# Soft-capped attention and a soft mixture of experts on one core: where casts, loads and weight transfers are placed

## The chip, the cores and the metric

The kernel runs on one core of a Trainium2 chip. Its engines are TensorE (PE, matmuls, with a weight-load row of its own, PEld), VectorE (DVE), ScalarE (ACT), GpSimd (POOL) and SyncE (SP), which here only issues DMAs. Matmuls write PSUM, everything else works on SBUF. The metric is device time of one execution in microseconds, the median over several runs. The profile comes from one further execution and has its own time.

## The reference

Attention with a soft cap on the scores, over q, k and v of shape (8, 12, 448, 64), then a soft mixture of 8 experts with 4 slots each over the 3584 resulting rows of 768:

```python
scores = cap * np.tanh((q @ k.T / 8) / cap)          # cap = 30
attn = softmax(scores, axis=-1)
x = (attn @ v) as (3584, 768)
logits = x @ phi                                      # phi (768, 32)
d = softmax(logits, axis=0)                           # over all rows
slots = (d.T @ x) as (8, 4, 768)
h = np.maximum(slots[e] @ w1[e], 0)                   # w1 (8, 768, 1024)
slot_out[e] = h @ w2[e]                               # w2 (8, 1024, 768)
out = softmax(logits, axis=1) @ slot_out              # (3584, 768), f32
```

All inputs are float32; the kernel's matmuls work on bfloat16.

## The kernel before, in words

**Units.** A quad is four heads of one batch element (24 quads, Q = 0 to 23); a pair is two heads (48), and each pair has 7 tiles (64 keys of each of its two heads against 448 queries), so 336 tiles. A chunk j holds 6 tiles (56 chunks), a half chunk 3. Seven chunks make one batch element, called b, with three quads 3b, 3b+1, 3b+2.

**The order is written out by hand.** Each engine runs its instructions in the order in which the Python code issues them. The loop at L451 runs over the chunks. In chunk j ScalarE does two tanh (`tanh_chunk`, L243, one for each half chunk) and the exp of the chunk before (`exp_chunk`, L247); TensorE does the scores of the next chunk (`qk_chunk`, L236, two half chunks, into two PSUM buffers) and the probability-times-V passes of an earlier pair (`pv_pass`, L264, two halves), normalized by VectorE (`norm`, L274 and L275). One chunk in seven has no P·V pass. Between these stand the slots "0", "a", "b", "c", "d", in which `run` calls whatever `at(j, slot, f, ...)` has entered:

- `cast` (L194): VectorE turns a float32 q or k quad into bfloat16, and then SP issues the load of the next quad into the same buffer (`load`, L153; one buffer each for q, k and v).
- `transp` (L204, L206): seven TensorE transposes into the one buffer of `psT` and a VectorE copy out.
- `vcast` (L214, L215): GpSimd casts v into one of two buffers `vbd`, and SP issues the next v load.
- `x_transp`, `logits`, `slot_sums`, `e_transp`, `e_norm`, `e_sums`: the mixture's logits and slot sums of finished batch elements.
- `spare(n)`: n junk matmuls, whose result nobody reads, into the P·V buffer (one buffer).
- `load_w1`, `load_w2`: GpSimd issues a weight DMA that casts float32 to bfloat16. 24 jobs bring w1 into SBUF (512 KB each as bfloat16, three per expert), 6 bring the first 24 blocks of w2 into SBUF (768 KB), and 10 bring the other 40 blocks into a bfloat16 copy in DRAM, `w2d` (768 KB). They are entered at equal distances in chunks, L421.

`quad_in` (L386) enters the five steps of a quad: cast k, cast q, transpose k, transpose q, cast v.

**Start.** `load_first` issues quad 0 in halves, then v of quad 0, then k, q, v of quad 1 into an area that a w1 tile uses later. 33 junk matmuls run, then `first_half(0)` casts and transposes the first pair of quad 0, `qk_chunk(0)` follows, then `first_half(1)` and `qk_chunk(1)`.

**End.** After the last exp the attention's SBUF pools are closed and the tiles `w2t` (L535 to L539) take their place: 20 DMAs on SP's queue bring `w2d` back, each as soon as the attention tile under it is free. The built program gives SP eight completion semaphores in turn, so a DMA also waits for the landing of the one eight before. Layer 1 (L552), its transposes (`h_transp`) and layer 2 (L579) follow. Layer 2 takes 64 blocks for the first 384 output columns (half 0), casts the sums (L618), then 64 blocks for the second half, with five output tiles' first halves between (`half_tile`, L604), and casts these (L626). Then come the output matmuls (L642), scaled by VectorE or ScalarE (L646, L648) and stored (L594).

Of the kernel before, what the change touches and what calls it, by code (L numbers as in the profile page):

```python
# [9 lines left out]
BF16 = mybir.dt.bfloat16  # L10
# [4 lines left out]
P = 128  # L15
HP = 64
NT = 7
# [6 lines left out]
VW = 2 * (DH + 1)  # L24
# [4 lines left out]
def kernel(  # L29
# [12 lines left out]
    B, H, _, _ = q.shape  # L42
    D = H * DH
    E = moe_w1.shape[0]
    F = moe_w1.shape[2]
    NS = moe_phi.shape[1]
    NJ = D // P
    NFT = F // P
    cap = float(cap)
    qk_scale = 1.0 / (DH ** 0.5)  # L50
# [5 lines left out]
    NCH = NTILE // CH  # L56
    R2 = 24

    ctx.enter_context(tc.manual_schedule())
    pe, dve, act, pool, sp = nc.tensor, nc.vector, nc.scalar, nc.gpsimd, nc.sync  # L60
# [15 lines left out]
    pool.memset(mask[0:HP, NG - 1, :], MASKED)  # L76
    phib = consts.tile([P, NJ, NS], BF16, name="phib")
    ET4 = consts.tile([P, B // 2, NT, 2, HP], BF16, name="ET4")
    winv = consts.tile([P, B // 2, NT], F32, name="winv")
    hpad = consts.tile([P, E, NFT, NS], BF16, name="hpad")  # L80
    slT = consts.tile([P, NJ, NS], BF16, name="slT")
    zacc = consts.tile([P, 1], F32, name="zacc")
    rz = consts.tile([P, 1], F32, name="rz")
    slacc = consts.tile([P, NJ, NS], F32, name="slacc")

    w1b = [wts.tile([P, NJ, F], BF16, name=f"w1b{e}", tag="w1", bufs=E)
           for e in range(E - 1)]
    w2b = wts.tile([P, R2, D], BF16, name="w2b")


    blocks = [(i, ft, gg) for i in range(E // 4) for ft in range(NFT) for gg in range(4)]

    def w2_src(n0, n):

        i, ft, gg = blocks[n0]
        return bass.AP(tensor=moe_w2.tensor,
                       offset=((4 * i + gg) * F + ft * P) * D,
                       ap=[[D, P], [F * D, n], [1, D]])
# [8 lines left out]
    def load_w2(dst, n0):  # L107
        pool.dma_start(out=dst, in_=w2_src(n0, 4))

    wjobs = [(load_w1, e, jh) for e in range(E) for jh in range(NJ // 2)]  # L110
    wjobs += [(load_w2, w2b[:, n0:n0 + 4, :], n0) for n0 in range(0, R2, 4)]

    dram = ctx.enter_context(tc.tile_pool(name="dram", bufs=1, space=bass.MemoryType.DRAM))
    w2d = []
    for n0 in range(R2, len(blocks), 4):
        t = dram.tile([P, 4, D], BF16, name=f"w2d{n0}")
        wjobs.append((load_w2, t, n0))
        w2d.append(t)

    att = ExitStack()  # L120
# [1 line left out]
    cst = att.enter_context(tc.tile_pool(name="cst", bufs=1))  # L122
    ldv = att.enter_context(tc.tile_pool(name="ldv", bufs=1))
    qk = att.enter_context(tc.tile_pool(name="qk", bufs=2))
    vb = att.enter_context(tc.tile_pool(name="vb", bufs=1))
    exps = att.enter_context(tc.tile_pool(name="exps", bufs=4))
    xs = att.enter_context(tc.tile_pool(name="xs", bufs=4))
    attp = ExitStack()
    psS = attp.enter_context(tc.tile_pool(name="psS", bufs=2, space=PSUM))
# [3 lines left out]
    raws, casts, qkT = {}, {}, {}  # L133
# [3 lines left out]
    def quad_ap(nm, Q, h=None):  # L137
        b, hq = divmod(Q, NQB)
        off = (b * H + 4 * hq) * S * DH
        if h is not None:  # L140
            return bass.AP(tensor=srcs[nm].tensor, offset=off + 2 * h * S * DH,
                           ap=[[NT * DH, P], [1, NT * DH]])
        return bass.AP(tensor=srcs[nm].tensor, offset=off,
                       ap=[[NT * DH, P], [2 * S * DH, 2], [1, NT * DH]])
# [11 lines left out]
    def load_first():  # L156

        for nm in "qkv":
            raws[nm, 0] = raw_tile(nm)
        for h in range(2):  # L160
            sp.dma_start(out=raws["q", 0][:, h, :], in_=quad_ap("q", 0, h))
            act.dma_start(out=raws["k", 0][:, h, :], in_=quad_ap("k", 0, h))
        sp.dma_start(out=raws["v", 0], in_=quad_ap("v", 0))
        t = wts.tile([P, 3, 2, S], F32, name="raw1", tag="w1", bufs=E)
        for n, nm in enumerate("kqv"):
            raws[nm, 1] = t[:, n, :, :]
            sp.dma_start(out=raws[nm, 1], in_=quad_ap(nm, 1))

    def first_half(h):

        for nm in ("q", "k"):
            if h == 0:
                casts[nm, 0] = cst.tile([P, NT, P], BF16, name=nm + "bf", tag=nm + "bf")
                qkT[nm, 0] = qk.tile([P, NT, P], BF16, name=nm + "T", tag=nm + "T")
            dve.tensor_copy(
                casts[nm, 0][:, :, h * HP:(h + 1) * HP]
                .rearrange("p c (a d) -> p a c d", a=2),
                raws[nm, 0][:, h, :].rearrange("p (c a d) -> p a c d", a=2, d=DH // 2))
        for nm in ("q", "k"):
            ps = (psT if nm == "q" else psV).tile(  # L180
                [P, NT, P], BF16, name=nm + "ps", tag="T" if nm == "q" else "pv")
            r = slice(h * HP, h * HP + HP)
            for c in range(NT):
                pe.transpose(ps[r, c, :], casts[nm, 0][:, c, r], ident)
            cuts = (0, 2, NT) if (nm, h) == ("k", 0) else (0, NT)
            for c0, c1 in zip(cuts, cuts[1:]):
                dve.tensor_copy(qkT[nm, 0][r, c0:c1, :], ps[r, c0:c1, :])
            if h == 1:
                raws.pop((nm, 0)), casts.pop((nm, 0))
                load(nm, 2)  # L190
# [15 lines left out]
        dve.tensor_copy(t, ps)  # L206
        qkT[nm, Q] = t

    vbds = [vb.tile([P, 2, NT, VW], BF16, name=f"vbd{n}") for n in range(2)]

    def vcast(Q):
        raw = raws.pop(("v", Q)).rearrange("p h (c d) -> p h c d", d=DH)
# [14 lines left out]
    def qk_chunk(i):  # L227
        sc = psS.tile([P, CS, 512], F32, name="sc", tag="sc")
        scores[i] = sc
        for u in range(CS):  # L230
            pr, c = divmod(i * CS + u, NT)
            Q, h = divmod(pr, 2)
            r = slice(h * HP, h * HP + HP)
            for n in range(2):
                cs = slice(n * HP, n * HP + HP)
                pe.matmul(sc[cs, u, 0:S], qkT["k", Q][r, c, cs],  # L236
                          qkT["q", Q][r, :, cs], start=True, stop=True)
# [136 lines left out]
    def at(j, slot, f, *a):  # L374
        if j < 0:
            j, slot = 0, "b"
        aux.setdefault((j, slot), []).append((f, a))

    def spare(n):

        busy(n, psV.tile([P, 2, VW], F32, name="junk", tag="pv")[:, 0, 0:P])
# [4 lines left out]
    def quad_in(Q, cast_k, cast_q, k_in, q_in, v_in):  # L386
        if 0 < Q < NQ:
            at(*cast_k, cast, "k", Q)
            at(*cast_q, cast, "q", Q)
            at(*k_in, transp, "k", Q)  # L390
            at(*q_in, transp, "q", Q)
            at(*v_in, vcast, Q)

    for b in range(B):
        j = b * PER
        quad_in(3 * b + 1, (j - 1, "d"), (j, "a"), (j, "b"), (j, "c"), (j + 2, "c"))
        quad_in(3 * b + 2, (j + 1, "c"), (j + 1, "d"), (j + 2, "b"), (j + 2, "c"),
                (j + 5, "c"))
        quad_in(3 * b + 3, (j + 3, "d"), (j + 4, "c"), (j + 5, "b"), (j + 5, "c"),
                (j + 7, "c"))  # L400
        p = 6 * b
        at(j + 2, "a", spare, 12)
        at(j + 4, "a", x_transp, p)
        at(j + 5, "a", x_transp, p + 1)
        at(j + 6, "a", x_transp, p + 2)
        at(j + 5, "d", logits, 3 * b)
        if b < B - 1:
            at(j + 7, "a", x_transp, p + 3)
            at(j + 8, "a", x_transp, p + 4)
            at(j + 7, "d", logits, 3 * b + 1)  # L410
            at(j + 9, "a", x_transp, p + 5)
            at(j + 9, "d", logits, 3 * b + 2)
            at(j + 11, "0", e_exp, b)
            at(j + 11, "d", slot_sums, b)
            at(j + 12, "d", e_transp, b)
            at(j + 13, "d", e_norm, b)
            if b % 2:
                at(j + 14, "d", e_sums, b // 2)
    nw = len(wjobs)
    for n, job in enumerate(wjobs):  # L420
        at(1 + n * (NCH - 5) // nw, "b", *job)  # L421

    def run(j, slot):
        for f, a in aux.pop((j, slot), []):
# [12 lines left out]
    init_vbd()  # L437
    first_half(0)
    qk_chunk(0)
    first_half(1)  # L440
    qk_chunk(1)
    at(1, "b", vcast, 0)
    at(3, "b", dve.memset, hpad, 0.0)
    pool.dma_start(out=phib, in_=moe_phi.rearrange("(jt ji) s -> ji jt s", ji=P))
# [87 lines left out]

    tl = ctx.enter_context(tc.tile_pool(name="tl", bufs=1, reuse_waits="tile"))

    w2t = []  # L535
    for n0 in range(R2, len(blocks), 2):
        t = tl.tile([P, 2, D], BF16, name=f"w2t{n0}")
        sp.dma_start(out=t, in_=w2d[(n0 - R2) // 4][:, (n0 - R2) % 4:(n0 - R2) % 4 + 2, :])
        w2t.append(t)  # L539

    def w2_block(n):
        return w2b[:, n, :] if n < R2 else w2t[(n - R2) // 2][:, (n - R2) % 2, :]

    hbs = {}

# [24 lines left out]
                      ap=[hpad.ap[0], [NS, NFT], [NFT * NS + 4, 4], [1, 4]])  # L570
        dve.tensor_copy(dst, src)

    HD = D // 2
    so_ps = []

    def layer2(n0, half):
        for n in range(n0, n0 + 4):
            i, ft, gg = blocks[n]
            pe.matmul(so_ps[half][32 * gg:32 * gg + NS, :],  # L579
                      hpad[:, 4 * i + gg, ft, :],  # L580
                      w2_block(n)[:, half * HD:(half + 1) * HD],
                      start=(n0 == 0), stop=(n0 == len(blocks) - 4))

    layer1(0, 0, e_norm)
# [46 lines left out]
    for n in range(B // 2 * NT):  # L631
        bb, c = divmod(n, NT)
# [52 lines left out]
```

## Time and profile before

| | |
|---|---|
| median of 7 runs | 339.37 us (334.57 to 344.61) |
| profiled execution, whole | 337.23 us |
| its span, first to last instruction | 335.4 us |
| mean granted TensorE clock in it | 0.885 |
| ScalarE tanh, L243 | x112, 145.4 us busy, 1409 ns mean |
| ScalarE exp, L247 | x57, 144.0 us busy, 2546 ns mean |
| TensorE P·V, L264 | x1288, 98.6 us busy |
| TensorE scores, L236 | x672, 87.7 us busy |
| TensorE idle before score matmuls, for a PSUM buffer that ScalarE reads | 13.0 us in 24 waits |
| VectorE idle before q casts, for q loads | 4.4 us |
| DMA of w1, w2 (SBUF), w2 (DRAM) | x24, x6, x10; median 8.6, 10.7, 11.5 us to landing |
| DMA of q, k, v | x22, x22, x23; median 6.1, 5.6, 7.8 us to landing |
| reload of w2 from DRAM | x20, 384 KB each, median 5.8 us to landing |
| stores of whole output tiles | x23, 384 KB each, median 4.3 us to landing |

Durations on ScalarE include the overlap of an instruction with the one behind it, so two tanh and one exp together advance the timeline by 4.67 us a chunk, less than the sum of their means. In the slices of the page each character is 8.4 us: a digit is a share in tenths, and PEclk is the granted clock of TensorE, which in this execution is either 1.00 or 0.50 at any moment. In timelines the bracket at the end of a row tells how long the engine was idle before it and what ended that.

### The profile page before, as it was taken

How to read it: one execution, taken by the hardware profiler on the slowest of the kernel's cores; microseconds unless marked ns; L12 is line 12 of the kernel's file. 1: busy time of each engine (PE TensorE's matmuls, PEld its weight loads, DVE VectorE, ACT ScalarE, POOL GpSimd, SP SyncE). 2: the span in 40 equal slices, each digit the busy share in tenths (PEclk: the TensorE clock that was granted, in tenths of full speed). 3: DMA queues.
4: the chain of work that ended last, by engine and by line, in shares of the span. 5: the costliest groups of instructions: out<-in, count | busy, mean ns of one | idle time of the engine just before them, and what ended most of it. 6: DMA issues, size and time to landing. Idle time of an engine off the chain costs nothing.

```text
span 335.4 us, 8116 instructions
## 1 busy us (share of the span) xinstructions
PE 279.2 (83%) x3486; PEld 187.7 (56%) x3486; DVE 173.9 (52%) x426; ACT 282.5 (84%) x199; POOL 84.5 (25%) x107
## 2 busy tenths in 40 slices
PE   7789987999799887888998878978997887978680
PEld 6346664676557665665576556755665657533220
DVE  6624664356436654565366545754675345216542
ACT  2688999989979999999999999999999997203450
POOL 5500442234044231430442143341430220000000
PEclk9557999579959999999599999999899999989855
DMA  8992699394978995969799999999999553945998
GB/s 266 264 274 94 156 243 267 76 280 105 257 202 189 197 250 191 229 169 241 214 227 241 287 277 213 261 259 267 289 231 226 187 166 93 359 196 202 394 399 322
DMA packets 43044, 77.65 MB, mean 231 GB/s; under 512 B 3456, under 2 KB 31360, under 8 KB 43008
## 3 DMA queue, kind: packets, MB, share of 16 engines
q1 hardware_dynamic: 26960, 51.45, 43.8%
q0 software_dynamic: 15760, 25.22, 42.6%
q8 instruction: 27, 0.44, 0.5%
q10 hardware_dynamic: 288, 0.46, 0.4%
q14 instruction: 9, 0.07, 0.1%
HBM read 91.32 MB, written 18.87 MB: 329 GB/s over the span
## 4 chain that ended last, share of the span: by engine, by line
ACT 48%; PE 30%; DMA 9%; DVE 8%; issue 1%; SPq 1%; DVEq 0%; ACTq 0%
ACT ex L243 24%; ACT ex L247 23%; PE pv L264 8%; PE sc L236 8%; DMA qraw<-in_q_dram 5%; DMA out_dram<-ob 2%; DMA w2t<-w2d 2%; PE kps L204 2%; PE qps L204 2%; DVE kT L206 2%; PE so_ps L579 1%; PE hp L552 1%; PE boot L434 1%; SPq L594 1%; DVE xq L275 1%
## 5 line engine op out<-in xcount | busy, mean ns | idle before, releaser
L243 ACT ACTIVATE ex<-sc 128x1344 bf16<-128x1344 f32 x112 | 145.4, 1409 | 13.4 <-PE sc L236 10.7
L247 ACT ACTIVATE ex<-ex 128x2688 bf16<-128x2688 bf16 (+1 forms) x57 | 144.0, 2546 | 0.0
L264 PE MATMUL pv<-vbd,ex 128*128 128x130 bf16 x1288 | 98.6, 231 | 4.9 <-ACT ex L247 2.3
L264 PEld LDWEIGHTS <-ex 128*128 128x128 bf16 x1344 | 85.2, 103 | 26.3 <-DVE xq L275 17.1
L236 PE MATMUL sc<-qT,kT 64*64 64x448 bf16 x672 | 87.7, 395 | 13.4 <-ACT ex L243 13.0
L214 POOL CAST vbd<-vraw 64x896 bf16<-64x896 f32 x23 | 21.7, 944 | 147.1 <-DMA vraw<-in_v_dram 89.3
L274 DVE RECIPROCAL rec<-pv 128x4 f32<-128x4 f32 x92 | 16.8, 182 | 69.3 <-PE pv L264 69.3
L236 PEld LDWEIGHTS <-kT 64*64 64x64 bf16 x672 | 29.1, 111 | 34.5 <-issue 19.1
L275 DVE TENSOR_TENSOR xq<-pv,rec 128x256 bf16<-128x256 f32 x92 | 39.0, 424 | 3.2
L215 POOL CAST vbd<-vraw 64x896 bf16<-64x896 f32 x23 | 26.1, 1136 | 1.3
L206 DVE COPY kT<-kps 128x896 bf16<-128x896 bf16 x23 | 14.3, 622 | 16.4 <-PE kps L204 16.3
L194 DVE CAST qbf<-qraw 128x896 bf16<-128x896 f32 x22 | 19.1, 869 | 4.4 <-DMA qraw<-in_q_dram 4.4
L204 PE MATMUL qps<-ident,qbf 128*128 128x128 bf16 x161 | 14.1, 233 | 7.3 <-DVE kT L206 7.2
L292 DVE COPY xT<-xps 128x512 bf16<-128x512 bf16 x47 | 19.5, 415 | 1.0 <-PE xps L290 1.0
L290 PE MATMUL xps<-ident,xq 128*128 128x128 bf16 x188 | 18.5, 221 | 0.7 <-DVE zacc L329 0.7
L642 PE MATMUL op<-so,ET 128*128 128x384 bf16 x46 | 14.7, 416 | 4.8 <-DVE ob L646 3.4
L204 PEld LDWEIGHTS <-kbf 128*128 128x128 bf16 x161 | 10.8, 102 | 13.7 <-issue 8.6
L206 DVE COPY qT<-qps 128x896 bf16<-128x896 bf16 x23 | 14.3, 620 | 7.5 <-PE qps L204 7.2
L204 PE MATMUL kps<-ident,kbf 128*128 128x128 bf16 x161 | 13.9, 231 | 5.0 <-DVE xT L292 3.8
L648 ACT ACTIVATE ob<-op,winv 128x768 f32<-128x768 f32 x11 | 9.9, 900 | 9.5 <-DMA out_dram<-ob 8.0
L318 POOL COPY e<-E 128x512 bf16<-128x512 bf16 x8 | 4.9, 608 | 51.6 <-ACT E L312 36.1
L204 PEld LDWEIGHTS <-qbf 128*128 128x128 bf16 x161 | 12.0, 104 | 9.4 <-issue 9.0
(94 smaller groups left out, 224.2 us busy)
## 6 DMA issues: line engine op xcount, KB each, us to landing
w1b<-in_moe_w_dram POOLq DMA_DIRECT2D x24, 512.0 KB, 8.6
vraw<-in_v_dram SPq DMA_DIRECT2D x23, 448.0 KB, 7.8
qraw<-in_q_dram SPq DMA_DIRECT2D x22, 448.0 KB, 6.1
kraw<-in_k_dram SPq DMA_DIRECT2D x22, 448.0 KB, 5.6
out_dram<-ob SPq DMA_DIRECT2D x23, 384.0 KB, 4.3
w2d<-in_moe_w_dram POOLq DMA_DIRECT2D x10, 768.0 KB, 11.5
w2t<-w2d SPq DMA_DIRECT2D x20, 384.0 KB, 5.8
w2b<-in_moe_w_dram POOLq DMA_DIRECT2D x6, 768.0 KB, 10.7
```

The costliest lines, as they stand in the source:

```text
L194: dve.tensor_copy(t.rearrange("p c (h d) -> p h c d", h=2), raws.pop((nm, Q)).rearrange("p h (c d) -> p h c d", d=DH))
L204: pe.transpose(ps[:, c, :], src[:, c, :], ident)
L206: dve.tensor_copy(t, ps)
L214: pool.tensor_copy(t[0:HP, :, :, 0:DH], raw[0:HP])
L215: pool.tensor_copy(t[HP:P, :, :, DH + 1:VW - 1], raw[HP:P])
L236: pe.matmul(sc[cs, u, 0:S], qkT["k", Q][r, c, cs], qkT["q", Q][r, :, cs], start=True, stop=True)
L243: act.activation(exs[j][:, half * CS:half * CS + CS, :], scores.pop(i)[:, :, 0:S], ACT.Tanh, scale=qk_scale / cap)
L247: act.activation(exs[j][:, u0:u1, :], exs[j][:, u0:u1, :], ACT.Exp, scale=cap)
L264: pe.matmul(pvs[pr, half][:, n, 0:VW], exs[j][:, u, GOFF[g]:GOFF[g] + P], vbds[Q % 2][:, h, c, :], start=(c == 0 and n == 0), stop=(c == N ...
L275: dve.tensor_tensor(xq[Q][:, 2 * half:2 * half + 2, h * P:(h + 1) * P] .rearrange("p g (i d) -> p g i d", i=2), pv[:, :, :, 0:DH], rec.to_ ...
L290: pe.transpose(ps[:, g, :], xq[Q][:, g, h * P:(h + 1) * P], ident)
L292: dve.tensor_copy(t, ps)
```

## The change

- The start issues `qk_chunk(1)` ahead of `first_half(1)`, with six junk matmuls behind it. Ten more junk matmuls stand in each of the slots (0, "c"), (0, "d"), (1, "a") and (1, "c").
- v of quad 0 is loaded after k and q of quad 1.
- The steps of the three quads of a batch element move. For quad 3b+2, for example, cast k stays at (j+1, "c"), cast q moves from (j+1, "d") to (j+2, "c"), transpose k stays at (j+2, "b"), transpose q moves from (j+2, "c") to (j+2, "d"), and the v cast from (j+5, "c") to (j+4, "d").
- Weight jobs get costs 4 (w1), 6 (w2 to SBUF) and 3 (half of a w2 job to DRAM), and are entered in proportion to the costs, from chunk 2 on and not from chunk 1.
- Each of the 10 jobs to DRAM becomes two, one for each half of the output columns, and `w2d` holds the halves apart. The reload takes all first halves, then all second halves: still 20 DMAs of 384 KB.
- The two `vbd` buffers get pools of their own, with the `exps` pool between them in SBUF.

```diff
+    def load_half(dst, n0, half):
+        src = w2_src(n0, 4)
+        pool.dma_start(out=dst, in_=bass.AP(tensor=src.tensor, offset=src.offset + half * HD,
+                                            ap=[[D, P], [F * D, 4], [1, HD]]))
...
     for n0 in range(R2, len(blocks), 4):
-        t = dram.tile([P, 4, D], BF16, name=f"w2d{n0}")
-        wjobs.append((load_w2, t, n0))
+        t = dram.tile([P, 2, 4, HD], BF16, name=f"w2d{n0}")
+        for half in range(2):
+            wjobs.append((load_half, t[:, half, :, :], n0, half))
         w2d.append(t)
...
-    vb = att.enter_context(tc.tile_pool(name="vb", bufs=1))
+    vb = [att.enter_context(tc.tile_pool(name="vb0", bufs=1))]
     exps = att.enter_context(tc.tile_pool(name="exps", bufs=4))
+    vb.append(att.enter_context(tc.tile_pool(name="vb1", bufs=1)))
...
-        sp.dma_start(out=raws["v", 0], in_=quad_ap("v", 0))
         t = wts.tile([P, 3, 2, S], F32, name="raw1", tag="w1", bufs=E)
         for n, nm in enumerate("kqv"):
             raws[nm, 1] = t[:, n, :, :]
+            if nm == "v":
+                sp.dma_start(out=raws["v", 0], in_=quad_ap("v", 0))
             sp.dma_start(out=raws[nm, 1], in_=quad_ap(nm, 1))
...
-        quad_in(3 * b + 1, (j - 1, "d"), (j, "a"), (j, "b"), (j, "c"), (j + 2, "c"))
-        quad_in(3 * b + 2, (j + 1, "c"), (j + 1, "d"), (j + 2, "b"), (j + 2, "c"),
-                (j + 5, "c"))
-        quad_in(3 * b + 3, (j + 3, "d"), (j + 4, "c"), (j + 5, "b"), (j + 5, "c"),
-                (j + 7, "c"))
+        quad_in(3 * b + 1, (j - 1, "b"), (j, "a"), (j - 1, "d"), (j, "c"), (j + 1, "d"))
+        quad_in(3 * b + 2, (j + 1, "c"), (j + 2, "c"), (j + 2, "b"), (j + 2, "d"),
+                (j + 4, "d"))
+        quad_in(3 * b + 3, (j + 4, "a"), (j + 5, "a"), (j + 4, "d"), (j + 5, "c"),
+                (j + 6, "d"))
...
-    nw = len(wjobs)
+
+    cost = [{load_w1: 4, load_w2: 6, load_half: 3}[job[0]] for job in wjobs]
     for n, job in enumerate(wjobs):
-        at(1 + n * (NCH - 5) // nw, "b", *job)
+        at(2 + sum(cost[:n]) * (NCH - 6) // sum(cost), "b", *job)
+    for j, slot in ((0, "c"), (0, "d"), (1, "a"), (1, "c")):
+        at(j, slot, spare, 10)
...
     qk_chunk(0)
+    qk_chunk(1)
+    spare(6)
     first_half(1)
-    qk_chunk(1)
...
-    w2t = []
-    for n0 in range(R2, len(blocks), 2):
-        t = tl.tile([P, 2, D], BF16, name=f"w2t{n0}")
-        sp.dma_start(out=t, in_=w2d[(n0 - R2) // 4][:, (n0 - R2) % 4:(n0 - R2) % 4 + 2, :])
-        w2t.append(t)
...
+    w2t = {}
+    for half in range(2):
+        for n0 in range(R2, len(blocks), 4):
+            t = tl.tile([P, 4, HD], BF16, name=f"w2t{n0}_{half}")
+            sp.dma_start(out=t, in_=w2d[(n0 - R2) // 4][:, half, :, :])
+            w2t[n0, half] = t
...
+    def w2_half(n, half):
+        if n < R2:
+            return w2b[:, n, half * HD:(half + 1) * HD]
+        return w2t[n - n % 4, half][:, n % 4, :]
```

## The prediction

> **What bounds the kernel now.** I read the page first, then ScalarE's timeline (the busiest engine), then the windows by granted clock, then the chain of waits behind chunk 55. From the page, busy shares and the 40 slices of 8.4 us:
>
> ```profile
> PE 279.2 (83%) x3486; PEld 187.7 (56%) x3486; DVE 173.9 (52%) x426; ACT 282.5 (84%) x199; POOL 84.5 (25%) x107
> ...
> ACT  2688999989979999999999999999999997203450
> ...
> PEclk9557999579959999999599999999899999989855
> ```
>
> ScalarE is full from slice 4 to slice 33 and light at both ends. Its need is fixed: 112 tanh at 1.18 us and 56 exp at 2.335 us are 263 us of the 335.4 us span. So the change can only win where ScalarE is not full: the start, a few holes, and the 56 us behind the last exp (279.8). Its holes in the timeline (in brackets: idle time before, and who ended it):
>
> ```profile
> 25.51 1.29 ACT L243 ACTIVATE ex<-sc 128x1344 bf16<-128x1344 f32 x1 [1.60 <-PE sc L236]
> ...
> 29.80 2.47 ACT L243 ACTIVATE ex<-sc 128x1344 bf16<-128x1344 f32 x2 [0.67 <-PE pv L264]
> ...
> 68.55 2.63 ACT L243 ACTIVATE ex<-sc 128x1344 bf16<-128x1344 f32 x2 [0.81 <-PE pv L264]
> ...
> 95.43 1.29 ACT L243 ACTIVATE ex<-sc 128x1344 bf16<-128x1344 f32 x1 [1.44 <-PE sc L236]
> ```
>
> With 0.21 at 75.1, 0.70 at 99.9 and 0.32 at 166.5 the holes after 29.8 sum to 0.81+0.21+1.44+0.70+0.32 = 3.5 us. From 7.38 to 29.80 ScalarE does 8 tanh and 3 exp, 16.4 of 22.4 us: 6.0 us lost at the start. Every hole has TensorE as releaser, and lies in or just behind a stretch of half clock (windows: length, busy times, PEclk third from the end):
>
> ```profile
> 26.33:29.74 3.41, 3.41 (x28) 2.28 (x25) 1.52 (x3) 2.80 (x2) 0.00 (x0) 0.50 0.04 15
> ...
> 53.63:57.05 3.42, 1.73 (x20) 1.09 (x19) 0.62 (x1) 3.42 (x3) 1.88 (x2) 1.00 1.08 265
> 57.05:70.70 13.65, 13.65 (x127) 8.75 (x126) 5.08 (x14) 12.79 (x10) 3.69 (x5) 0.50 0.62 155
> 87.77:91.18 3.41, 2.05 (x26) 1.37 (x23) 1.40 (x4) 3.41 (x4) 0.00 (x0) 1.00 1.07 267
> ```
>
> The clock halves behind a 3.4 us window in which TensorE is busy for 50 to 60% (1.73 and 2.05 of 3.41 us). At 87.8 a load is the cause: VectorE stands for q (issued at 82.56, landed 8.0 us later), so a transpose waits 1.50 us. At 53.6 it is chunk 9, one of those without a probability-times-V pass. The tail:
>
> ```profile
> 297.61 0.34 PE L579 MATMUL so_ps<-w2t,hpad 128*32 128x384 bf16 x2 [0.63 <-DMA w2t<-w2d]
> 298.56 0.34 PE L579 MATMUL so_ps<-w2t,hpad 128*32 128x384 bf16 x2 [0.61 <-DMA w2t<-w2d]
> 299.52 0.51 PE L579 MATMUL so_ps<-w2t,hpad 128*32 128x384 bf16 x2 [0.62 <-DMA w2t<-w2d]
> ...
> 305.88 0.56 DVE L626 CAST so<-so_ps 128x384 bf16<-128x384 f32 x1 [0.38 <-PE so_ps L579]
> ```
>
> Layer 2's first column half waits for the last reloaded weights, one every 0.96 us (393 KB, 410 GB/s). The idle window costs the clock again (0.50 from 299.4 to 302.8). From 310 to 330 the stores fill the DMA engines (share 1.01, 393 to 400 GB/s), so the end follows the time at which the layer-2 sums are ready.
>
> **The sum, part by part,** on the profiled run's 337.23 us (span 335.4 and 1.8 around it), which is 2.1 under the median of 339.37.
>
> *Reload by halves: the largest term.* Before, 8 of 20 reloads are issued by 277.7; the ninth waits for the last P·V matmul and goes at 283.59 (5.5 us of SP's waiting), and half 0 needs all 20. After, each of the 20 has the same 393 KB, but the first ten are all that half 0 needs. By the built program's waits eight still go by 277.7, the ninth waits for an exp and the first reload's landing (about 278, since vbd 1 now lies behind the exp buffers), the tenth for the last P·V (283.6); by the 3.1 us of the 283.59 reload it lands at 286.7. Half 0 starts at 293.09, so nothing is late. Eleven reloads from 283.6 at 0.96 us end at 286.7 + 9.6 = 296.3, with a slip as before (two waits for an earlier reload's landing, 2.8 us) 299; half 1 reaches its first reloaded block at 298.3 and its last near 301. Half 0: 32 of its 64 matmuls stand before the transpose and run unchanged; the other 32 start at 295.43 and take 32 x 0.048 (24 in 1.15) + 0.3 drain = 1.8, so its cast starts at 297.3 and not 300.06: -2.8. Half 1 takes 64 x 0.048 + 5 x 0.27 (output matmuls at full clock) + 0.3 = 4.7 at full clock, and the second cast starts at 301.9, not 305.88: -3.9. Stores are what is late next, and shift whole: **-3.9** (0 if a w2d write were late, -4.5 if the store ramp tightens).
>
> *Casts, transposes, loads spread.* No instruction is added. The gaps between q casts go from 1.75, 2.75, 2.5 chunks to 2.5, 2.5, 2.0; at 4.67 us a chunk the shortest goes from 8.2 to 9.3 us, k's are 10.5 and up. Loads of q and k land in 3.2 to 8.2 us, but for 9.7 and 10.3 near 191 and 224 and 11.7 at the start. So the q wait that costs 1.44 + 0.70 goes. The holes of chunk 9's kind stay: transposing k and q apart moves a 0.72 us wait for the kT copy behind a score chunk, but a P·V-free chunk keeps its idle time. V is cast a chunk sooner; POOL's cast waits there for the last reader of its buffer, and behind it only weight DMAs and the e copies queue. **-2.0** (0 to -3.5).
>
> *Weight DMAs by bytes.* w1 goes from one 512 KB job per 1.275 chunks to one per 1.04, w2 from 768 KB per 1.275 to per 1.56. Read rates, in f32, with 126 GB/s of q, k, v: 176+126 = 302 GB/s becomes 341 in the first half, 264+126 = 390 becomes 341 in the second. ScalarE had no hole under 390 GB/s (168 to 277 us), so 341 costs 0. Ten more jobs come from w2d:
>
> ```profile
> L108 POOL DMA_DIRECT2D w2d<-in_moe_w_dram x10: 697/702/908, 200.3 to 249.2; - x10
> ```
>
> They are 10 x 0.70 = 7 us of POOL, 25% busy, and delay only V casts, a chunk early. If they were exposed the bound is 7 us. Pieces written fall from 1536 to 768 bytes; no row has that, and I take 0, since the phase is spread over 15 chunks in place of 12. The Trainium skill ("DMA: Bandwidth & Descriptors", Anatomy of one DMA) speaks against the split: a fixed cost of about 2.0 us per GpSimd DMA. By it ten more would be an estimated 20 us, were they in line; the 0.70 us row with 7.9 us median landings, several in flight, says that they are not.
>
> *Start.* Score chunk 1 goes ahead of the second half-quad (only the first half is needed), then 6 junk matmuls, then 4 x 10 more. Junk takes the single P·V buffer, whose reader, the kT copy, is done by 6.91 for the first six; nothing else waits for it before chunk 3. Chunk 1 saves ScalarE 2.5 us at 11.20 but tanh 3 waits for chunk 3, behind quad 1's transposes:
>
> ```profile
> 12.55 0.93 PE L204 MATMUL kps<-ident,kbf 128*128 128x128 bf16 x7 [0.98 <-DVE kbf L194]
> 14.20 0.91 PE L204 MATMUL qps<-ident,qbf 128*128 128x128 bf16 x7 [0.71 <-DVE kT L206]
> 15.03 2.12 PE L236 MATMUL sc<-qT,kT 64*64 64x448 bf16 x12
> ...
> 19.00 1.46 PE L434 MATMUL junk<-ones 128*128 128x128 bf16 x12
> ```
>
> VectorE's chain sets 12.55. Its second-half casts take 1.13 us beside POOL's V casts (0.40 for the first half without them); the V load moves back, so POOL's casts move from there onto quad 1's casts (0.63 alone, 1.28 beside). I take 12.2. Ten junk matmuls cost 1.17 us at half clock (12 in 1.40), 0.69 at full (12 in 0.83). Now the clock decides. Half from 12.7 on: chunks 3, 4, 5 end at 16.4, 20.0, 22.4 and tanh 8 starts at 32.8 in place of 29.80, **+3**. Full throughout: 26.9, **-2.9**. Rows in between: the clock came back behind windows with 2.22 (26.33), 2.17 (98.01) and 1.94 us (67.28, with 0.65 of slot sums) of P·V matmuls, not behind 1.73 (63.87). The window from 16.1 gets 2.3 us of junk, full-array like these, before 0.97 at most. So I take a return at 17.5 to 20.8 by where windows fall: tanh 8 at 29.4, or 28.1 where the fall also comes a window later: **-1.0**.
>
> The Trainium skill ("TensorE: Matmul & The Clock Gate", Part 1) has full clock return after one busy window of about 3.4 us. By it the junk would win nearer to -2.9. The row 57.05:70.70 disagrees: busy throughout, half clock for four windows.
>
> Sum: -3.9 - 2.0 - 1.0 = -6.9, so 330.3 for the profiled run. Of its 2.1 us distance to the median I keep half, since I take part of the scatter (334.57 to 344.61) to be the same holes: 331.4, **331.5 us**.
>
> **Rivals.** (1) Junk without a return of the clock: +3 in place of -1, 335.5. For: two windows of 100% busy did not bring it back; against: they held few full-array matmuls. (2) The reload doesn't do it: the half-0 tail hangs on something else (a late w2d write of chunk 51, SP behind a V load): 331.5 + 3.9 = 335.4. Against: writes land within 13.6 us, 16 us ahead of need. (3) Slower: 39 GB/s more in the first half makes q and k loads later than their gap. VectorE is in order, so the cast blocks norms and the kT copies, TensorE idles, the clock halves: 2.1 us each, by the one at 91. Two such waits in each of the first four batches (the 2.0-chunk q gap, a 2.25-chunk k gap) make 16.8 us: 348. It decides once loads take over 9.3 us, and turns the sign at four such waits (6.9 / 2.1 = 3.3). For: 9.7 and 10.3 us were seen at 390 GB/s; against: there ScalarE had no hole. (4) Better: the clock never falls at the start, and chunk 9's kind of hole goes too: 328.
>
> **Numbers.** Forecast 0.58 (328 to 335), (1) 0.13, (2) 0.09, (3) 0.10, (4) 0.10. A measurement here tells 1% (3.4 us) from no change. Faster takes the forecast, (4) and 0.11 of (1) and (2), which stand at the edge of 336.0; same takes their other 0.11 and 0.02 of (3); slower the rest of (3). The range 327 to 338 leaves out (3) and the far ends of the others.
>
> **What would show it.** No DMA wait at layer 2 and the second cast near 302 less the shift before it (tail); no q-cast wait over 1 us on VectorE (spread); a return of the clock before 21 us, tanh 8 before 29.8 (start); w2d landings under 14 us. Wrong: cast waits for q or k in several batches, or half clock from 12 to past 26 us.

## The result, and the profile after

| | before | after |
|---|---|---|
| median of the runs | 340.38 us (331.83 to 345.91, 31 runs) | 329.92 us (326.60 to 335.53, 12 runs) |
| ratio after to before | | 0.9854, 95% interval 0.9800 to 0.9908 |
| profiled execution, whole (span) | 337.23 us (335.4) | 329.23 us (327.4) |
| start of tanh 8 | 29.80 | 29.95 |
| from there to the end of the last exp | 252.4 | 248.4 |
| from the end of the last exp to the end | 53.2 | 49.0 |
| mean granted TensorE clock | 0.885 | 0.932 |

The kernel is faster: the whole interval lies below 1. The ratio leaves out runs more than 1.5% above the fastest of their kernel, so it stands nearer to 1 than the quotient of the two medians, 0.969; of the profiled executions below, those of the start alone, the pacing alone, without the pacing and the six kept are such runs. Tanh 8 is counted from 0, as in the prediction, so it is ScalarE's ninth; the expectations below also call it the eighth. The three stretches differ by +0.15, -3.9 and -4.2 us, together the 8.0 us between the two profiled executions. Nothing was won at the start.

From the page, the busy shares and the slices of ScalarE and of the granted clock:

```profile
PE 269.9 (82%) x3532; PEld 185.0 (57%) x3532; DVE 169.3 (52%) x426; ACT 281.5 (86%) x199; POOL 90.2 (28%) x117
...
ACT  2669999999999999999999999999999999114440
...
PEclk9879999989979999999799997999999699999775
```

TensorE has 46 more matmuls and is busy 9.3 us less, because it runs longer at full clock. Between start and tail the clock now falls for one or two windows of 3.4 us at a time, where it fell for up to four (13.7 us at 57). ScalarE's timeline, with the idle time before a row in brackets:

```profile
12.44 1.27 ACT L252 ACTIVATE ex<-sc 128x1344 bf16<-128x1344 f32 x1
17.06 1.29 ACT L252 ACTIVATE ex<-sc 128x1344 bf16<-128x1344 f32 x1 [3.35 <-PE sc L245]
20.43 2.62 ACT L252 ACTIVATE ex<-sc 128x1344 bf16<-128x1344 f32 x2 [2.08 <-PE sc L245]
...
96.59 2.47 ACT L252 ACTIVATE ex<-sc 128x1344 bf16<-128x1344 f32 x2 [0.43 <-PE pv L273]
```

Behind tanh 8 one hole of 0.43 us is left, where there were 3.5 us. Ahead of it, behind the first tanh, stand two of 3.35 and 2.08 us, both for scores, in place of five that sum to 5.3 us. The windows there (length, then busy time and count of PE, PEld, DVE, ACT, POOL, then granted clock, DMA share, GB/s):

```profile
10.08:13.49 3.41, 1.13 (x11) 0.59 (x12) 2.72 (x4) 3.40 (x2) 3.23 (x4) 1.00 0.97 307
13.49:16.91 3.42, 3.12 (x23) 2.06 (x22) 1.57 (x3) 0.22 (x1) 2.82 (x4) 0.50 0.62 163
16.91:20.32 3.41, 3.35 (x29) 2.25 (x28) 0.00 (x0) 1.29 (x1) 0.00 (x0) 0.50 1.11 207
20.32:23.73 3.41, 3.41 (x45) 2.23 (x45) 0.01 (x1) 3.26 (x3) 0.00 (x0) 1.00 1.09 261
```

The clock fell behind a window busy for 33%, and came back at 20.32. ScalarE worked 0.22 and 1.29 us in the two windows between, in which TensorE was nearly full. Its rows show the junk in front of the scores that ScalarE's tanh at 17.06 and 20.43 wait for:

```profile
14.49 1.27 PE L446 MATMUL junk<-ones 128*128 128x128 bf16 x10
15.70 1.33 PE L245 MATMUL sc<-qT,kT 64*64 64x448 bf16 x6
16.96 2.53 PE L446 MATMUL junk<-ones 128*128 128x128 bf16 x20
19.42 0.95 PE L245 MATMUL sc<-qT,kT 64*64 64x448 bf16 x6
```

The tail, TensorE's and VectorE's rows:

```profile
291.64 1.49 PE L594 MATMUL so_ps<-w2t,hpad 128*32 128x384 bf16 x32 [0.32 <-DVE hpad L587]
...
298.51 0.66 PE L619 MATMUL op<-so,ET 128*128 128x384 bf16 x3 [0.72 <-DVE so L641]
...
297.89 0.56 DVE L641 CAST so<-so_ps 128x384 bf16<-128x384 f32 x1 [0.38 <-PE so_ps L594]
```

No matmul of layer 2 waits for a transfer any more; the second cast starts 19.5 us behind the last exp (23.7 before). The halved transfers and the loads of q:

```profile
qraw<-in_q_dram SPq DMA_DIRECT2D x22, 448.0 KB, 8.4
...
w2d<-in_moe_w_dram POOLq DMA_DIRECT2D x20, 384.0 KB, 9.4
```

The median q load takes 8.4 us to land (6.1 before): the loads did become slower, and still VectorE waits less for them, 3.4 us (4.4 before).

### The profile page after: what moved, and what is told of

Its sections match the earlier page's. It is cut to its first block, busy times and chain, and to the rows that moved or that the text cites. A ratio compares the mean times of both kernels' runs of the same rounds, so it can differ in the third digit from the quotient of the medians.

```text
span 327.4 us, 8212 instructions
## 1 busy us (share of the span) xinstructions
PE 269.9 (82%) x3532; PEld 185.0 (57%) x3532; DVE 169.3 (52%) x426; ACT 281.5 (86%) x199; POOL 90.2 (28%) x117
## 3 DMA queue, kind: packets, MB, share of 16 engines
q0 software_dynamic: 21040, 25.22, 46.2%
## 4 chain that ended last, share of the span: by engine, by line
ACT 68%; PE 18%; DMA 6%; DVE 4%; SPq 1%; issue 1%; DVEq 0%; ACTq 0%
ACT ex L252 34%; ACT ex L256 33%; DMA qraw<-in_q_dram 3%; PE sc L245 3%; PE pv L273 3%; DMA out_dram<-ob 3%; PE so_ps L594 2%; PE hp L568 2%; PE junk L446 2%; SPq L609 1%; PE boot L446 1%; PE op L657 1%; PE op L619 1%; DVE ob L661 1%; ACT ob L663 1%
## 5 line engine op out<-in xcount | busy, mean ns | idle before, releaser
L252 ACT ACTIVATE ex<-sc 128x1344 bf16<-128x1344 f32 x112 | 150.6, 1508 | 10.6 <-PE sc L245 10.1
L256 ACT ACTIVATE ex<-ex 128x2688 bf16<-128x2688 bf16 (+1 forms) x57 | 149.7, 2645 | 0.0
L273 PE MATMUL pv<-vbd,ex 128*128 128x130 bf16 x1288 | 95.4, 226 | 4.9 <-ACT ex L256 2.6
L273 PEld LDWEIGHTS <-ex 128*128 128x128 bf16 x1344 | 82.2, 100 | 28.7 <-DVE xq L284 19.0
L245 PE MATMUL sc<-qT,kT 64*64 64x448 bf16 x672 | 82.5, 373 | 15.0 <-ACT ex L252 13.9
L223 POOL CAST vbd<-vraw 64x896 bf16<-64x896 f32 x23 | 21.5, 933 | 127.4 <-PE pv L273 92.9
L245 PEld LDWEIGHTS <-kT 64*64 64x64 bf16 x672 | 27.8, 107 | 33.7 <-issue 15.7
L224 POOL CAST vbd<-vraw 64x896 bf16<-64x896 f32 x23 | 23.6, 1028 | 1.3
L301 DVE COPY xT<-xps 128x512 bf16<-128x512 bf16 x47 | 19.5, 415 | 1.0 <-PE xps L299 1.0
L213 PE MATMUL kps<-ident,kbf 128*128 128x128 bf16 x161 | 12.8, 219 | 5.8 <-DVE slacc L373 2.2
L105 POOL DMA_DIRECT2D w1b<-in_moe_w_dram x24 | 17.4, 729 | 0.0
L446 PEld LDWEIGHTS <-ones 128*128 128x128 bf16 x202 | 14.8, 113 | 3.4 <-issue 2.3
L661 DVE TENSOR_SCALAR ob<-op,winv 128x768 f32<-128x768 f32 x12 | 12.1, 1014 | 8.3 <-DMA out_dram<-ob 5.9
```

Source lines behind the costliest of these rows:

```text
L213: pe.transpose(ps[:, c, :], src[:, c, :], ident)
L223: pool.tensor_copy(t[0:HP, :, :, 0:DH], raw[0:HP])
L224: pool.tensor_copy(t[HP:P, :, :, DH + 1:VW - 1], raw[HP:P])
L245: pe.matmul(sc[cs, u, 0:S], qkT["k", Q][r, c, cs], qkT["q", Q][r, :, cs], start=True, stop=True)
L252: act.activation(exs[j][:, half * CS:half * CS + CS, :], scores.pop(i)[:, :, 0:S], ACT.Tanh, scale=qk_scale / cap)
L256: act.activation(exs[j][:, u0:u1, :], exs[j][:, u0:u1, :], ACT.Exp, scale=cap)
```

## The experiments

Each was timed in five rounds beside the kernel before on the same chip. The kernel before had medians of 339.39, 337.94 and 338.90 us beside the three groups, and 340.38 beside the changed kernel, which was not timed with the groups. So a difference of medians across groups can carry up to 2.4 us of this; where it matters, the ratios or the profiles are named beside it. None of these kernels leaves out a part of the computation. The theory: the reload wins about 4 us in the tail, the spread wins by shorter waits for loads, the pacing does nothing beside it, and the junk costs more than the clock that it buys. The rivals: the new start pays, or the gain comes from the pacing.

### One part alone, put into the kernel before

**Reload by halves alone:** the tiles `w2d`, `w2t`, `vbd` as in the change, the two halves of a job issued where the one job stood.

```diff
+    def load_two(t, n0):
+        for half in range(2):
+            load_half(t[:, half, :, :], n0, half)
...
-        wjobs.append((load_w2, t, n0))
+        wjobs.append((load_two, t, n0))
```

> The kernel before, with the reload by column halves alone (w2d written in halves, both at the place of the one job; vbd buffers split by the exp pool). Theory (each part works by itself, the tail is the largest): no wait of the layer-2 matmuls for w2t; from the last exp (before 279.8) to the end 51.4 us in place of 55.6; start and holes in ScalarE as before; 3.9 to 4.2 us off, about 1.2%. Rival (the tail's gain needs the earlier v casts or the pacing, since SP reaches the reloads behind the v loads and the w2d writes end late): a reload still waits, the tail stays over 54 us, under 1.5 us off.

Measured: 336.15 us (332.04 to 339.51), ratio 0.9894 (0.9789 to 0.9999). The tail took 49.6 us in place of 53.2, with no wait for a transfer at layer 2: -3.6, and the median is 3.2 below that of the kernel before. This is a little under the 3.9 to 4.2 expected, with the mechanism as predicted.

**The start alone:** the three parts of the new start, `load_first`, `qk_chunk(1)` ahead with six junk matmuls, and the four slots.

> The kernel before, with the start alone: score chunk 1 early, 46 junk matmuls, v of quad 0 loaded later; weight jobs as before from chunk 1. Theory (junk only buys back at the return of the clock what it costs): half clock from about 13 to about 20, tanh 8 between 28.8 and 30.5 as in both kernels (29.80 and 29.95), total within 1.5 us of before, tail 55.6. Rival (junk loses, and the gain of the change at the start comes from the weight jobs that start later): tanh 8 at 31 or later, up to 3 us slower. Second rival (junk wins): tanh 8 before 28, 2 us faster.

Measured: 345.85 us (335.23 to 348.92), a median 6.5 us above that of the kernel before; one run took 335.23 and the other five 342.76 or more, so no ratio came of it. In the profile, which is of one of the five (343.63 us), tanh 8 starts at 33.07 (29.80 before). Windows:

```profile
15.03:18.44 3.41, 3.35 (x26) 2.09 (x24) 1.06 (x2) 1.29 (x1) 1.40 (x3) 0.50 1.11 293
18.44:21.85 3.41, 3.41 (x28) 1.83 (x25) 0.10 (x1) 1.29 (x1) 0.00 (x0) 0.50 1.11 214
21.85:25.27 3.42, 3.42 (x26) 1.90 (x23) 0.00 (x0) 2.89 (x2) 0.00 (x0) 0.50 1.09 265
...
28.68:32.09 3.41, 3.41 (x28) 2.31 (x27) 1.49 (x3) 3.31 (x2) 0.00 (x0) 0.50 0.00 0
32.09:35.51 3.42, 3.42 (x31) 2.52 (x30) 1.17 (x4) 2.75 (x4) 0.00 (x0) 0.50 0.02 5
```

Three windows full of junk and scores did not bring the clock back; it came at 35.51. In this execution the prediction's rival of a start without a return came true.

**The spread alone:** the three `quad_in` calls of the change.

> The kernel before, with only the new places of casts, transposes and v casts. Theory (the holes behind late q loads go): ScalarE's holes after tanh 8 under 1.5 us in sum, against 3.5 in the profile before; 2 to 3 us off the total; tail 55.6. Rival (the holes go because weights come at an even pace): holes stay at 3 us or more, total as before within 1 us.

Measured: 329.73 us (328.82 to 334.93), ratio 0.9781 (0.9707 to 0.9855). The expectation was 2 to 3 us; the median is 9.7 us below that of the kernel before, and the ratio stands for 2.2%, about 7 us. By itself it does as much as the whole change. Its profile against that of before: start -3.7, middle -4.5, tail -0.2.

**The pacing alone:** costs 4 and 6, from chunk 2 on.

```diff
-        at(1 + n * (NCH - 5) // nw, "b", *job)
+        at(2 + sum(cost[:n]) * (NCH - 6) // sum(cost), "b", *job)
```

> The kernel before, with only the weight jobs paced by bytes, from chunk 2 on (w2 jobs to DRAM whole, cost 6 each). Theory (pacing is worth nothing by itself): total within 1 us of before, holes 2 to 5 us. Rival (pacing is what removes the holes and thins the scatter): holes under 1.5 us, 2 us or more off. Third possibility (39 GB/s more reads in the first half make q loads late while casts stand at their old places): 1 to 3 us slower.

Measured: 336.37 us (329.08 to 341.12), ratio 0.9861 (0.9770 to 0.9953). Its median is 3.0 lower than that of before, and the ratio rests on its three fastest runs of twelve; its profiled execution is no faster (339.08, with 9.6 us of q waits). None of the three expectations fits both.

These last two profiles are alike up to quad 2's k transpose (the waits for q of the first come later, from 153.7 on), and so show what the spread does at the start. TensorE's rows, first with the pacing alone (old places), then with the spread alone:

```profile
19.46 0.93 PE L204 MATMUL kps<-ident,kbf 128*128 128x128 bf16 x7
21.11 0.91 PE L204 MATMUL qps<-ident,qbf 128*128 128x128 bf16 x7 [0.72 <-DVE kT L206]
21.94 1.32 PE L236 MATMUL sc<-qT,kT 64*64 64x448 bf16 x6
```

```profile
19.53 0.93 PE L204 MATMUL kps<-ident,kbf 128*128 128x128 bf16 x7
20.39 1.33 PE L236 MATMUL sc<-qT,kT 64*64 64x448 bf16 x6
21.71 0.93 PE L204 MATMUL qps<-ident,qbf 128*128 128x128 bf16 x7
```

With q's transpose one slot later, a half chunk of scores runs in place of the wait for the kT copy and ahead of q's transposes. It comes 21.94 - 20.39 = 1.55 us earlier, and tanh 8 starts at 26.12 and not at 27.61: 1.5 us. The other 2.2 us to the 29.80 of before are not the spread's: the kernel with the pacing alone has the same transposes as before.

### One part of the change undone

**Without the new start:** `qk_chunk(1)` behind `first_half(1)`, no added junk (v of quad 0 still loaded later).

> The changed kernel with the old order at the start and without the 46 added junk matmuls (v of quad 0 still loaded later, weight jobs from chunk 2). Theory (the junk costs TensorE about as much as it saves or more; the spread alone reached tanh 8 at 26.1): tanh 8 between 26 and 28, total 326 to 327.5, under both kernels. Rival (the junk is neutral and tanh 8 is set by where the clock windows fall): tanh 8 near 30 here too in one or the other run, total 329 to 331 as with junk. Second rival (junk gains): 331 or more.

Measured: 326.21 us (325.47 to 329.56), ratio 0.9753 (0.9685 to 0.9821). **Without the junk alone** (`qk_chunk(1)` stays ahead):

```diff
-    spare(6)
...
-    for j, slot in ((0, "c"), (0, "d"), (1, "a"), (1, "c")):
-        at(j, slot, spare, 10)
```

> The changed kernel without the 46 added junk matmuls, score chunk 1 still early. If the junk is what costs: like the kernel with the old start, 326 to 327.5, tanh 8 at 26 to 28. If the early chunk 1 is what costs (it stands before the second half-quad's transposes, 0.76 us of TensorE on VectorE's chain): 1 us slower than the old start. If neither: as the changed kernel, 329 to 331.

Measured: 326.45 us (324.93 to 329.94), ratio 0.9741 (0.9676 to 0.9806). Both start tanh 8 at 26.0, so the early score chunk is worth nothing, and the 46 junk matmuls cost 29.95 - 26.01 = 3.9 us at the start of the profiled executions and 329.92 - 326.45 = 3.5 us by the medians. ScalarE's rows without them:

```profile
13.97 2.47 ACT L252 ACTIVATE ex<-sc 128x1344 bf16<-128x1344 f32 x2 [0.85 <-PE sc L245]
16.68 1.29 ACT L252 ACTIVATE ex<-sc 128x1344 bf16<-128x1344 f32 x1 [0.23 <-PE sc L245]
...
26.01 2.47 ACT L252 ACTIVATE ex<-sc 128x1344 bf16<-128x1344 f32 x2 [0.93 <-PE pv L273]
```

The clock fell at 11.56 here and came back only at 25.22, five microseconds later than with the junk. Still the holes are 2.0 us and not 5.4. The first six junk matmuls have a price of their own. In the changed kernel they put the second half-quad's transposes back, and VectorE's casts of quad 1 then meet GpSimd's V casts. First the changed kernel, then the one without junk:

```profile
11.08 1.38 DVE L203 CAST kbf<-raw 128x896 bf16<-128x896 f32 x1
...
10.73 1.24 POOL L224 CAST vbd<-vraw 64x896 bf16<-64x896 f32 x1
```

```profile
9.81 0.62 DVE L203 CAST kbf<-raw 128x896 bf16<-128x896 f32 x1
...
9.96 1.26 POOL L223 CAST vbd<-vraw 64x896 bf16<-64x896 f32 x1 [7.22 <-DVE qbf L203]
```

With junk, the cast starts 0.35 us behind a cast of GpSimd's and takes 1.38 us; without, it starts 0.15 us ahead of GpSimd's first and takes 0.62. Quad 1's first transpose stands at 12.51 and at 10.49.

**Without the spread:** the old `quad_in` calls in the changed kernel.

> The changed kernel with casts, transposes and v casts at their old places. Theory (the spread is the largest term, since alone it took 9 us): 5 to 8 us slower than the changed kernel, 335 to 338, with q-cast waits on VectorE of 6 us or more in sum and ScalarE holes over 4 us. Rival (in the whole change the even weight pace already removes the holes): within 2 us of the changed kernel.

Measured: 336.92 us (332.99 to 342.83), ratio 0.9991 (0.9934 to 1.0049): 7.0 us above the changed kernel by the medians, 1.4% by the ratios (0.9991 against 0.9854), with the other three parts in it. Between the profiled executions 4.6 us lie in the middle (253.0 us against 248.4). Its profile shows the chain in the middle of the run. VectorE, TensorE and ScalarE in the timeline, then the windows:

```profile
56.26 0.63 DVE L203 CAST qbf<-qraw 128x896 bf16<-128x896 f32 x1 [3.67 <-DMA qraw<-in_q_dram]
...
57.27 0.90 PE L213 MATMUL kps<-ident,kbf 128*128 128x128 bf16 x7 [1.93 <-DVE xT L301]
...
61.10 1.29 ACT L252 ACTIVATE ex<-sc 128x1344 bf16<-128x1344 f32 x1 [1.86 <-PE sc L245]
```

```profile
53.90:57.31 3.41, 0.79 (x7) 0.40 (x7) 0.96 (x2) 3.41 (x3) 0.00 (x0) 1.00 0.89 303
57.31:60.72 3.41, 2.70 (x20) 1.70 (x19) 1.25 (x2) 1.93 (x2) 2.52 (x3) 0.50 0.58 170
```

The cast waits 3.67 us for q, the xT copy stands behind it on VectorE, TensorE's transposes behind that; TensorE is busy for 0.79 of 3.41 us, the clock halves, and ScalarE loses 1.86 us and 0.69 more at 65.6.

**Without the pacing:** equal distances from chunk 1 on, both halves of a job together.

> The changed kernel with weight jobs at equal distances from chunk 1 as before (both halves of a w2 job together). Theory (once casts are spread, pacing is worth nothing): within 1 us of the changed kernel, 329 to 331. Rival (the pace is needed: 390 GB/s of reads in the second half make the loads late for a 2.0-chunk gap): 2 us or more slower, with holes behind chunk 28.

Measured: 329.39 us (325.11 to 332.50, and one run of 773.8), ratio 0.9772 (0.9673 to 0.9871). That is 0.5 us from the changed kernel's median, and the profiled middles are alike (248.2 and 248.4 us): beside the spread the pacing is worth nothing that can be measured. One thing stays open. In the kernels with junk, tanh 8 came later where the weight jobs begin at chunk 1 (33.07 with the start alone, 31.05 here) than where they begin at chunk 2 (29.77 without the spread, 29.95 in the changed kernel). These are single executions, in which the clock also returned later (35.51 and 22.34 against 19.76 and 20.32); without junk there is no such difference (26.12 and 26.15 against 26.0).

### How much junk, and where

**20 for 10 in each of the four slots.**

> The changed kernel with 20 junk matmuls in place of 10 in each of the four slots (0, c), (0, d), (1, a), (1, c); nothing of the computation changes. Theory one, that junk stands in front of scores on the path: 30 of the 40 added matmuls are ahead of the score chunks that ScalarE waits for at 17.06 and 20.43, at 0.127 us each at half clock that is up to 3.8 us, so the eighth tanh goes from 29.96 to about 32 to 34 and the time from 329.9 to 332 to 334. Rival, that 10 are too few to bring the clock back: with 20 the clock returns a window earlier, the eighth tanh comes before 29 and the time falls to 329 or less.

Measured: 332.69 us (330.09 to 334.95), ratio 0.9859 (0.9796 to 0.9922). The median is 2.8 us above the changed kernel's, in the range of theory one, but the ratios of the two are alike (0.9859 and 0.9854), and tanh 8 came at 30.68, short of the 32 to 34 expected. ScalarE's rows, then the windows:

```profile
17.53 1.29 ACT L252 ACTIVATE ex<-sc 128x1344 bf16<-128x1344 f32 x1 [3.83 <-PE sc L245]
20.60 1.29 ACT L252 ACTIVATE ex<-sc 128x1344 bf16<-128x1344 f32 x1 [1.77 <-PE sc L245]
22.49 1.29 ACT L252 ACTIVATE ex<-sc 128x1344 bf16<-128x1344 f32 x1 [0.60 <-PE sc L245]
```

```profile
13.37:16.79 3.42, 3.04 (x29) 2.84 (x30) 1.66 (x3) 0.34 (x1) 2.90 (x4) 0.50 0.73 165
16.79:20.20 3.41, 3.35 (x53) 2.60 (x52) 0.00 (x0) 1.29 (x1) 0.00 (x0) 1.00 1.12 209
```

The rival was right about the clock, which came back one window earlier, at 16.79; even so ScalarE lost a little more. Of the 5.6 us between the two profiled executions only 0.7 lie at the start; 3.7 lie in the middle, with a hole of 1.31 at 120.2, and 1.2 in the tail. What the junk has to do with those is open.

**The six kept, the four slots empty.**

> The changed kernel with the six junk matmuls of the start kept and the 40 of the four slots left out. Theory one: the 40 make most of the loss. The first quad-1 transpose stays late (11.5 to 12.5, since the six hold up the second half-quad by 0.5 us and VectorE's quad-1 casts then fall on GpSimd's V casts), but the eighth tanh comes at 26.5 to 27.5 and the time is 326.5 to 327.5. Rival, that the six and the collision behind them make the loss: the eighth tanh stays at 28.5 or later and the time at 329 or more.

Measured: 327.32 us (322.57 to 330.45), ratio 0.9644 (0.9558 to 0.9731), which rests on its fastest runs. By the medians the 40 cost 2.6 us and the six 0.9, which is within the scatter; by tanh 8 of the profiles the 40 cost 2.1 and the six 1.8. Tanh 8 came at 27.84, 0.3 above the range, since the clock fell at 10.9 and returned only at 31.4. The collision is there, as expected (VectorE's k cast at 9.98 takes 1.35 us, and the transpose stands at 11.40).

**14 in an idle gap, the 46 left out.**

```diff
+    at(0, "b", spare, 14)
     for b in range(B):
         j = b * PER
```

> The changed kernel without its 46 junk matmuls, and with 14 in front of quad 1's k transpose, where TensorE idles (the clock window from 8.15 to 11.56 was busy for 50% there, and the clock fell behind it). Theory one, that the fall follows a window of 50 to 60% and that junk pays where it fills an idle gap ahead of the fall: this window comes to about 78%, the clock holds, scores of chunks 3 to 5 run at 0.11 us each in place of 0.17 to 0.22, ScalarE's holes of 0.85, 0.23 and 0.93 us go, the eighth tanh comes at 24.5 to 25.5 and the time is 325 to 326. Rival, that junk costs wherever it stands: the transpose comes 0.5 to 1 us later, the clock falls all the same, the eighth tanh at 26.5 or later, 327 to 328.

Measured: 325.83 us (323.18 to 329.33), ratio 0.9645 (0.9583 to 0.9706); tanh 8 at 26.30. Windows:

```profile
8.82:12.24 3.42, 2.24 (x27) 1.37 (x26) 2.73 (x5) 3.39 (x3) 2.52 (x2) 1.00 1.15 363
12.24:15.65 3.41, 1.86 (x22) 1.11 (x23) 1.91 (x3) 2.76 (x4) 3.29 (x5) 1.00 0.62 190
15.65:19.06 3.41, 3.41 (x24) 1.72 (x20) 0.00 (x0) 3.34 (x3) 0.71 (x2) 0.50 1.07 182
```

Half of theory one holds: a window busy for 2.24 of 3.42 us kept the clock, one window longer than without the junk. The next, at 1.86 (54%), lost it, and nothing was won at the start; the 0.6 us below the kernel without junk is within the scatter.

### The two parts that pay, together

**Spread and reload in the kernel before, nothing else.**

> The kernel before with the spread of casts and loads and the reload by halves (both halves of a DRAM job issued at the old job's place), without the new start and without the pacing. If the terms add up as the single runs say (the spread alone -9.7 on the medians, the reload -3.6 of the tail) it takes 325.5 to 327, the tail from the last exp is 49 to 50 and the eighth tanh is at 26 to 27. If pacing by bytes is worth anything beside the spread, this one is slower than the changed kernel without junk (326.45) by over 1 us.

Measured: 325.72 us (324.32 to 327.96), ratio 0.9662 (0.9603 to 0.9720); profile: tanh 8 at 26.15, tail 49.05. The parts add up as expected. This kernel beats both the kernel before and the changed one: its interval lies wholly below that of the changed kernel, and its median is 4.2 us lower. Beside the kernel without the new start (326.21, tanh 8 at 26.00), which has the pacing and the later load of v, it shows no worth in either.

## Why the prediction was right, and where it was not

The time lies in the range, 1.6 us under the forecast, and no rival came to pass as a whole; of rival (4) one half did, that holes of chunk 9's kind go. The gain was 10.5 us by the medians, 8.0 between the profiled executions and 1.5%, about 5 us, by the ratio, against 7.9 forecast. Of the four terms two are off, in opposite directions. The profiled execution was put at 330.3 us and took 329.23, since 1.9 us too little for the spread's middle stands against 1.15 too much for the start: that the sum came so close is in part luck.

| term | predicted | profiled execution | alone or undone |
|---|---|---|---|
| reload | -3.9 | -4.2 (tail) | -3.6 (tail, alone) |
| spread | -2.0 | -3.9 (middle) | -9.7 (median, alone), +7.0 (median, undone; 4.6 in the middle) |
| pacing | 0 | | none told apart (329.39 undone against 329.92) |
| start | -1.0 | +0.15 | +3.7 (329.92 against 326.21 without it; 3.95 in the profiles) |

*Reload.* Right in mechanism and size. The second cast was put at 301.9 less the shift before it; the shift is 282.2 - 278.4 = 3.8, and 297.89 + 3.8 = 301.7. Over all profiles, four tails with whole reloads have a mean of 52.8 us and ten with halves 49.4.

*Spread.* The mechanism was right, the size was not: "**-2.0** (0 to -3.5)" was worked out from the holes of one execution. "So the q wait that costs 1.44 + 0.70 goes" takes one long wait for the rule. The profiled execution of before had the mildest waits of the five kernels with the old places:

| profiles | VectorE's wait for q loads | tanh 8 to end of last exp |
|---|---|---|
| five with the old places | 4.4 to 12.8, mean 8.7 us | 252.4 to 256.8, mean 254.5 us |
| nine with the new places | 0.1 to 4.7, mean 2.9 us | 247.9 to 252.1, mean 249.3 us |

So the middle wins 5.2 us by the means; without the four executions named with the result the means are 253.1 and 249.5, and it wins 3.6. No run parts the wider gap between q casts from the moved transposes and v casts: that the gap does it is read from the waits and from the chain at 56.26, not tested alone. The sum carried half of the 2.1 us to the median for the scatter; all of it, and more, was due (10.5 us between the medians, 8.0 between the profiles). The second failing of this step is at the start: "transposing k and q apart moves a 0.72 us wait for the kT copy behind a score chunk" was given no price, and is worth 1.5 us where ScalarE runs dry. That no q wait over 1 us would be left was wrong too; one of 1.68 us is there, at 91.4, with the hole of 0.43 behind it. The holes "of chunk 9's kind", which were to stay, are gone from the changed kernel's profile. Of the 9.7 us of the spread alone these two make 5.1 to 6.7; the rest is not divided further.

*Pacing.* Right beside the spread (0.5 us). Alone it has a ratio of 0.9861, which no profile explains; it stays open. The Trainium skill ("DMA: Bandwidth & Descriptors", Anatomy of one DMA) has a fixed cost of about 2.0 us for each GpSimd DMA, most of it in the completion, by which the ten added ones would have cost an estimated 20 us in line. The runs show a median of 0.73 us of GpSimd each and of 9.4 us to landing, several in flight, and no loss that can be measured.

*Start.* Here the prediction failed: "So I take a return at 17.5 to 20.8 by where windows fall: tanh 8 at 29.4, or 28.1". The clock did return in that span, at 20.32, and fell a window later than before; yet tanh 8 came at 29.95, and not before 29.8 as the prediction's own sign asked. Two things were left out. The step asked only whether another instruction waits for the junk's buffer, and charged the six nothing; alone they put tanh 8 from 26.01 to 27.84: VectorE's cast falls on GpSimd's, the transposes come 0.9 us later (11.40 against 10.49), and the clock came back later too. And it compared with one start of before, 29.80, as if that were fixed. With the old places and no new junk tanh 8 came at 29.80, 29.00 and 27.61; with the new places and none at 26.00 to 26.15 in four profiles. The right question was what the start would be with the spread alone. Against 26.0 the junk loses 4.0 us in the profile, because ten and twenty matmuls at half clock stand in front of scores that ScalarE needs, and the clock that they buy comes when most of that is lost. The spread's 1.5 us and a milder start hid this in the comparison with before. The rival "junk without a return of the clock" was priced at +3 on the start of before; against the start without junk the loss was 3.9 even with a return.

The Trainium skill ("TensorE: Matmul & The Clock Gate", Part 1: The HAM clock gate) has full clock after one busy window of about 3.4 us, and half clock after an idle one. Neither holds here: three windows at 98 to 100% in the start-alone kernel did not bring full clock, and it was lost behind windows with 0.79 to 1.86 of 3.41 us busy, none of them idle.

## What to carry to other kernels

One profile is one draw: where waits for loads scatter from run to run, size a term by several executions, or carry the whole distance between the profiled run and the median. Junk that is meant to hold a clock is paid for where it stands in front of an instruction that the busiest engine waits for; price every single one on the path, and compare with the start that the other edits already give. On an engine that works in order, a cast that waits for a load holds up everything behind it, so the spread, which widens the shortest gap between loads, was worth more here (9.7 us alone, by the medians) than the reload by halves (3.2).

## What the runs showed of the hardware

- The fall of the clock follows the busy time of a 3.41 us window. Over all fourteen profiles, up to 275 us, each full-clock window with TensorE busy for up to 1.86 us (54%) was followed by half clock and none with more than 2.60 us (76%); between these both occur.
- The return does not go by busy time alone. It came behind a window of 3.04 us (89%), with 20 junk matmuls, seven transposes and hardly a score, and not behind three of 3.35 to 3.42 us full of scores and junk. No half-clock window returned whose time went to scores for more than 1.67 us (49%), and none that was busy for less than 3.03 us (89%). Two full windows with 1.42 and 1.43 us of scores and 1.73 and 1.70 us of P·V went different ways: half clock stayed at 63.87 in the kernel before, and full clock came at 93.88 without the new start. What decides is open.
- A VectorE cast of 128x896 from float32 takes 0.62 us when it starts 0.15 us ahead of a GpSimd cast, and 1.38 us when it starts 0.35 us behind one. The half-quad casts took 1.13 us in the profile of before (6.84, GpSimd's at 6.69) and 0.38 with the pacing alone (6.40, GpSimd's at 6.71). A few tenths of a microsecond in the order decide over 0.75. Over all fourteen profiles 132 VectorE casts of 128x896 began while a GpSimd cast ran, and 130 of them ended 0.48 to 0.61 us behind that cast's end, however early they had begun: they waited for it.
